# Part of wq in whole runs, eight partitions to a transfer, and the last piece of wo in two transfers

## Chip, cores, metric

The kernel runs on one core of a Trainium2 chip. The metric is the device time of one execution in microseconds, the median of several runs.

## The reference, cut to what matters

One decode step for a batch of 8: attention over the last 1,024 positions of a cache (16 query heads, 8 key/value heads, 256 wide), an MLP, and a gate that mixes the two.

```python
W = min(4096, max(256, Sk // 4))                 # 1024 of 4096 positions
q = (x @ wq) -> (B, Hq, 1, Dh)                   # x: 8 x 448, wq: 448 x 4096
k, v = last W positions, repeated for 2 query heads per kv head
o = softmax(q k^T * Dh**-0.5) v                  # per batch and head
a = o.reshape(B, Sq, Hq*Dh) @ wo                 # wo: 4096 x 448
b = gelu(layernorm(x) @ w1 + b1) @ w2 + b2
out = g * a + (1 - g) * b                        # g = sigmoid(sum(x * gate_w))
```

Everything is bf16. Keys and values alone are 64 transfers' worth of 1 MB; all weights together are some 10 MB.

## The kernel before

The order of work is written out by hand. Nearly all loads are issued by the sync engine (SP), in this order: w1 (L159, L162), w2 (L164), wq in three pieces (L167), the rest of wq (L168), and then the units of the list built at L170 to L179: a transfer of K or V for two batches of one kv head (1 MB, `load`, L148), and after each head's four K transfers the piece of wo that belongs to the head (448 KB, L187). Keys run ahead of values. The list ends with the last values and, as its last transfer, the piece of wo for the last head. The very last V transfer goes in two halves (L145). x, two biases and the gate's vector are issued by the scalar engine (L156 to L158, L288).

wq is 448 rows of 4,096 numbers. Its first 384 rows lie in `wq_sb` as 128 partitions of three rows: partition p holds rows 3p, 3p+1 and 3p+2, which are one run of 24,576 B in memory. Before, one transfer carries row c of every partition: 128 runs of 8,192 B, three transfers.

TensorE first makes the MLP's two products, then q (L377): for c = 0, 1, 2 and the rest, 32 small matmuls each, over all 128 partitions of `wq_sb[:, c]`. Then follows a software pipeline over 64 steps of half a K transfer each: transpose the keys (L407, copied out of PSUM by VectorE at L412), scores (L433), softmax once per head (L446 to L496), the values' product (L508), and per head the output product with wo (L533), which adds into one PSUM bank. For each head the output product takes the first query head's two blocks of wo, then the second's. At the end the last output product, one VectorE instruction (L577) and two stores (L581).

A pool of 12 buffers holds keys and values. The trace shows eight semaphore numbers on the loads, used in turn.

Of the kernel before, what the change touches and what calls it, by code (L numbers as in the profile page):

```python
# [16 lines left out]
def kernel(  # L17
# [15 lines left out]
    nc = tc.nc  # L33
    P = nc.NUM_PARTITIONS

    B, Sq, D = A_x.shape
    _, Hkv, Sk, Dh = A_k_cache.shape
    HD = A_wq.shape[1]
    Hq = HD // Dh
    rep = Hq // Hkv  # L40
# [4 lines left out]
    NJ = Dh // P  # L45
# [61 lines left out]
    NKH = rep * NJ  # L107
    wq_sb = big.tile([P, DC, HD], BF16, name="wq_sb")
    wq_t = big.tile([P, HH], BF16, name="wq_t")
    w1_sb = big.tile([P, DC, F], BF16, name="w1_sb")  # L110
    wo_sb = [big.tile([P, NKH, D], BF16, name=f"wo_sb{g}") for g in range(Hkv)]
# [29 lines left out]
    def load(kind, n):  # L141
        t = kvpool.tile([P, NC, Dh], BF16, tag="kv", name="kv")
        src = A_k_cache if kind == "K" else A_v_cache
        g, u = divmod(n, NBU)
        parts = TB if (kind, n) == ("V", NU - 1) else 1  # L145
        w = NC // parts
        for q in range(parts):
            nc.sync.dma_start(  # L148
                t[:, q * w : (q + 1) * w, :].rearrange("p c d -> p (c d)"),
                src[u * TB : (u + 1) * TB, g, kv0:Sk, :].rearrange(  # L150
                    "t (r c) d -> r t c d", c=NC
                )[:, :, q * w : (q + 1) * w, :].rearrange("r t c d -> r t (c d)"),
            )
        KV[kind, n] = t
# [8 lines left out]
    w2_v = w2_sb[:].rearrange("p (h k) n -> p h k n", h=2)  # L163
    nc.sync.dma_start(w2_v, B_w2.rearrange("(h p k) n -> p h k n", h=2, k=NH))  # L164
    wq_v = A_wq[0:DM, :].rearrange("(p c) n -> p c n", c=DC)
    for c in range(DC):
        nc.sync.dma_start(wq_sb[:, c, :], wq_v[:, c, :])  # L167
    nc.sync.dma_start(wq_t[:], A_wq[DM:D, :].rearrange("r (h n) -> (r h) n", h=2))  # L168

    VU = (SPG + LAG) // TB  # L170
# [11 lines left out]
    def issue_to(k):  # L182
        while pos[0] < len(units):
            kind, n = units[pos[0]]
            if kind == "W":
                r0 = n * NKH * P
                nc.sync.dma_start(  # L187
                    wo_sb[n][:].rearrange("p (i j) n -> p i (j n)", i=rep),
                    A_wo[r0 : r0 + NKH * P, :].rearrange(
                        "(i p j) n -> p i (j n)", i=rep, j=NJ  # L190
                    ),
                )
            else:
                if pos[1] == k:
                    return
                load(kind, n)
                pos[1] += 1
            pos[0] += 1

    issue_to(NKV)  # L200


# [343 lines left out]
    for n in range(LAST):  # L546
        if n < NSTEP:
            transposes(n)
            done += n % TB == TB - 1
        if 0 <= n - 1 < NSTEP:  # L550
            scores(n - 1)
        g, r = divmod(n, SPG)
        if g >= 1 and g - 1 < Hkv:
            if r == 0:
                soft_max1(g - 1)
            if r == 1:
                soft_max2(g - 1)
            if r == 2:
                soft_exp(g - 1)
        m = n - SPG - LAG  # L560
        if m >= 0:
            pv(m)
            if m % SPG == 1:
                soft_sum(m // SPG)
            if m == SPG:
                gate_load()
            if m == 2 * SPG:
                gate()
            done += m % TB == TB - 1
            if m % SPG == SPG - 1:  # L570
                o_scale(m // SPG)
            if m % SPG == 0 and m > 0:
                o_proj(m // SPG - 1)
        issue_to(NKV + done)
# [37 lines left out]
```

## Time and profile before

| what | value |
|---|---|
| median of 3 runs | 196.78 us (196.78 to 196.85) |
| the profiled execution: its time | 196.92 us |
| its span, first to last instruction | 195.2 us |
| moved by the DMA engines | 78.14 MB, 400 GB/s over the span |
| TensorE (PE) matmul busy | 164.2 us (84%) |
| VectorE (DVE) busy | 113.1 us (58%) |
| ScalarE (ACT) busy | 6.4 us (3%) |
| mean granted TensorE clock | 0.768 |

The profile gives, for each line of the kernel, the busy time and what an engine waited for; the span in 40 slices of 4.88 us with the share of the 16 DMA engines that were busy; the chain of waits that ended last; and for each window asked for, the busy time of each engine and the DMA share. Behind these views lie records of each DMA packet (start, length, bytes, queue) and of each landing: a transfer posts one landing on its semaphore for each DMA engine that carried a share of it.

### The profile page before, as it was taken

To read this page: it belongs to the slowest core of one execution; us is meant where nothing else is said; L and a number is where in the kernel's file an instruction comes from. 1 tells how busy PE (TensorE), PEld (TensorE's weight loads), DVE (VectorE), ACT (ScalarE), POOL (GpSimd) and SP (SyncE) were. 2 spreads that over 40 slices of the span, in tenths; PEclk is the share of its full clock that TensorE was granted. 3 is DMA by queue.
4 is the path that set the end of the run, shared out by engine and by line. 5 is a ranking of instruction groups with operands and counts; after the bars stand their busy time and mean duration, and the time that the engine had idled before them with its cause. 6 is when DMAs were issued, how large, how long until landed. Compare 5 with 4: busy or idle time off the path is not lost.

```text
span 195.2 us, 7355 instructions
## 1 busy us (share of the span) xinstructions
PE 164.2 (84%) x3417; PEld 153.6 (79%) x3417; DVE 113.1 (58%) x255; ACT 6.4 (3%) x13; POOL 2.8 (1%) x16
## 2 busy tenths in 40 slices
PE   2677799988899796958999898988898989989752
PEld 1565799988899796957999797978897989989541
DVE  3122189996477653764559674964586646766401
ACT  5000000000000000010000000000000000000000
POOL 5000000000000000000000000000000000000000
PEclk9999889997569855585569996995599655699555
DMA  6999999999999999999999999999999999999940
GB/s 215 412 426 425 425 413 426 426 423 420 421 426 422 417 425 426 425 417 431 423 423 419 422 425 428 418 421 418 425 430 417 421 425 430 426 420 425 394 176 5
DMA packets 12769, 78.14 MB, mean 400 GB/s; under 512 B 1330, under 2 KB 3523, under 8 KB 4164
## 3 DMA queue, kind: packets, MB, share of 16 engines
q1 hardware_dynamic: 12688, 77.67, 95.4%
q8 instruction: 26, 0.43, 0.8%
q10 hardware_dynamic: 52, 0.02, 0.0%
q14 instruction: 3, 0.02, 0.0%
HBM read 77.68 MB, written 0.01 MB: 398 GB/s over the span
## 4 chain that ended last, share of the span: by engine, by line
DMA 91%; PE 6%; SPq 1%; issue 0%; DVE 0%
DMA kv<-in_A_k_cache_dram 47%; DMA kv<-in_A_v_cache_dram 19%; DMA wo_sb<-in_A_wo_dram 18%; DMA wq_sb<-in_A_wq_dram 7%; PE ktp L407 4%; PE grp L433 1%; PE A_bank L533 0%; PE grp L508 0%; SPq L167 0%; PE grp L422 0%; SPq L164 0%; DVE res L577 0%; SPq L159 0%; SPq L162 0%; SPq L148 0%
## 5 line engine op out<-in xcount | busy, mean ns | idle before, releaser
L412 DVE COPY kt<-ktp 128x1024 bf16<-128x1024 bf16 x128 | 84.4, 687 | 44.4 <-PE ktp L407 43.9
L407 PE MATMUL ktp<-ident,kv 128*128 128x128 bf16 x1024 | 89.0, 257 | 7.9 <-DMA kv<-in_A_k_cache_dram 6.7
L407 PEld LDWEIGHTS <-kv 128*128 128x128 bf16 x1024 | 78.0, 118 | 10.9 <-DMA kv<-in_A_k_cache_dram 7.9
L508 PE MATMUL grp<-e,kv 128*128 128x4 bf16 x1024 | 35.6, 166 | 2.6 <-DMA kv<-in_A_v_cache_dram 2.5
L508 PEld LDWEIGHTS <-kv 128*128 128x128 bf16 x1024 | 32.6, 101 | 5.6 <-DMA kv<-in_A_v_cache_dram 2.8
L433 PE MATMUL grp<-qT,kt 128*128 128x4 bf16 x1024 | 36.6, 166 | 0.3 <-DVE kt L412 0.2
L433 PEld LDWEIGHTS <-kt 128*128 128x128 bf16 x1024 | 34.6, 100 | 1.8 <-issue 0.6
L482 ACT ACTIVATE e<-grp 128x256 bf16<-128x256 f32 x8 | 3.1, 383 | 161.8 <-PE grp L475 161.8
L491 PE MATMUL A_bank<-zs,onesf 128*128 128x16 f32 x16 | 3.6, 299 | 4.5 <-DVE zs L487 4.5
L491 PEld LDWEIGHTS A_bank<-zs,onesf 128*128 128x128 f32 x16 | 2.8, 218 | 5.1 <-DVE zs L487 5.1
L533 PE MATMUL A_bank<-wo_sb,ot 128*8 128x224 bf16 x64 | 5.5, 305 | 0.8 <-DMA wo_sb<-in_A_wo_dram 0.5
L321 PE MATMUL h_ps<-yT,w_sb 128*128 128x8 bf16 x42 | 4.2, 195 | 1.2 <-DMA w_sb<-in_B_w_dram 1.2
L495 DVE RECIPROCAL rz<-A_bank 128x16 f32<-128x16 f32 x8 | 2.1, 258 | 5.4 <-PE A_bank L491 5.4
L519 DVE TENSOR_TENSOR ot<-grp,rz 128x32 bf16<-128x32 f32 x8 | 1.5, 186 | 6.4 <-PE grp L508 6.4
L487 DVE TENSOR_REDUCE zs<-e 128x16 f32<-128x256 bf16 x8 | 4.8, 602 | 0.0
L353 PE MATMUL b_ps<-w_sb,hT 128*8 128x224 bf16 x28 | 2.8, 388 | 2.4 <-DVE b_ps L349 2.4
L338 DVE COPY z<-h_ps 128x112 f32<-128x112 f32 x1 | 0.3, 275 | 7.7 <-PE h_ps L329 7.7
L321 PEld LDWEIGHTS <-w_sb 128*128 128x128 bf16 x42 | 3.6, 152 | 1.3 <-DMA w_sb<-in_B_w_dram 1.3
L475 PE MATMUL grp<-diag,onesb 128*128 128x256 bf16 x8 | 2.5, 308 | 2.2 <-DVE diag L469 1.9
L353 PEld LDWEIGHTS <-hT 128*8 128x8 bf16 x28 | 1.8, 121 | 3.0 <-DVE hT L344 2.2
L446 DVE TENSOR_REDUCE pm<-grp 128x16 f32<-128x256 f32 x8 | 3.3, 415 | 0.6 <-PE grp L433 0.6
L533 PEld LDWEIGHTS <-ot 128*8 128x8 bf16 x64 | 2.6, 93 | 1.3 <-issue 0.4
(82 smaller groups left out, 53.6 us busy)
## 6 DMA issues: line engine op xcount, KB each, us to landing
kv<-in_A_k_cache_dram SPq DMA_DIRECT2D x32, 1024.0 KB, 18.3
kv<-in_A_v_cache_dram SPq DMA_DIRECT2D x31, 1024.0 KB, 18.3
wo_sb<-in_A_wo_dram SPq DMA_DIRECT2D x8, 448.0 KB, 18.3
wq_sb<-in_A_wq_dram SPq DMA_DIRECT2D x3, 1024.0 KB, 12.1
w_sb<-in_B_w_dram SPq DMA_DIRECT2D x1, 1568.0 KB
w_sb<-in_B_w_dram SPq DMA_DIRECT2D x1, 1344.0 KB, 5.9
kv<-in_A_v_cache_dram SPq DMA_DIRECT2D x2, 512.0 KB, 19.8
wq_t<-in_A_wq_dram SPq DMA_DIRECT2D x1, 512.0 KB, 14.5
```

What stands on the lines that cost most here:

```text
L321: nc.tensor.matmul(o, lhsT=cols(w1_sb[:, c, h * FH : (h + 1) * FH]), rhs=yT[:, c, :], start=(c == 0), stop=False,)
L353: nc.tensor.matmul(b_ps[CP * j : CP * j + NB, 0:DN], lhsT=M["hT"][:, k * NB : (k + 1) * NB] if k < NF else onesb[0:1, 0:NB], rhs=w2_sb[:, ...
L407: nc.tensor.transpose(ktp[:, c * P : (c + 1) * P], K[:, h * HC + c, j * P : (j + 1) * P], ident[:],)
L412: nc.vector.tensor_copy(kt[:, j, :], ktp[:])
L433: nc.tensor.matmul(G[g][:, s : s + RU], lhsT=kt[:, j, c * P : (c + 1) * P], rhs=qT[:, j, g, bu * TB : (bu + 1) * TB, :].rearrange("p t i - ...
L446: nc.vector.reduce_max(pm[:], G[g][:, S0 : S0 + NC * R].rearrange("p (c r) -> p r c", r=R), axis=AXIS.X,)
L475: nc.tensor.matmul(G[g][:, S0 : S0 + NC * R].rearrange("p (c r) -> p c r", c=NC), lhsT=onesb[:], rhs=diag[g % 2][:].unsqueeze(1).to_broadc ...
L482: nc.scalar.activation(e[:], G[g][:, S0 : S0 + NC * R], ACT.Exp)
L487: nc.vector.reduce_sum(zs[:], E[g][:].rearrange("p (c r) -> p r c", r=R), axis=AXIS.X)
L491: nc.tensor.matmul(zc, lhsT=onesf[:], rhs=zs[:], start=False, stop=True, skip_group_check=True)
L508: nc.tensor.matmul(G[g][:, o : o + RU], lhsT=V[:, cc, :].rearrange("p (q j) -> p j q", j=NJ)[:, j, :], rhs=E[g][:, cc * R + bu * RU : cc * ...
L533: nc.tensor.matmul(A_bank[CP * j : CP * j + NB, 0:DN], lhsT=ot[:].rearrange("p j (b i) -> p j i b", i=rep)[:, h, i, :], rhs=wo_sb[g][:, k, ...
```

## The change

Of the 128 partitions of `wq_sb`, the last 48 (80 to 127) are loaded in six transfers of eight partitions, each partition as its whole run of 24,576 B (196,608 B to a transfer). Two of these go ahead of each of the three transfers that carry row c, which now carry it for partitions 0 to 79 only. The piece of wo for the last head is issued as two transfers, one per query head, where it was one. The bytes that are loaded and where they lie in SBUF stay the same.

```diff
     wq_v = A_wq[0:DM, :].rearrange("(p c) n -> p c n", c=DC)
+    SH = 48
+    PM = P - SH
+    small = [(p, p + 8) for p in range(PM, P, 8)]
     for c in range(DC):
-        nc.sync.dma_start(wq_sb[:, c, :], wq_v[:, c, :])
+        for lo, hi in small[2 * c : 2 * c + 2]:
+            nc.sync.dma_start(
+                wq_sb[lo:hi].rearrange("p c n -> p (c n)"),
+                wq_v[lo:hi].rearrange("p c n -> p (c n)"),
+            )
+        nc.sync.dma_start(wq_sb[0:PM, c, :], wq_v[0:PM, c, :])
     nc.sync.dma_start(wq_t[:], A_wq[DM:D, :].rearrange("r (h n) -> (r h) n", h=2))
...
             if kind == "W":
                 r0 = n * NKH * P
-                nc.sync.dma_start(
-                    wo_sb[n][:].rearrange("p (i j) n -> p i (j n)", i=rep),
-                    A_wo[r0 : r0 + NKH * P, :].rearrange(
-                        "(i p j) n -> p i (j n)", i=rep, j=NJ
-                    ),
+                dst = wo_sb[n][:].rearrange("p (i j) n -> p i (j n)", i=rep)
+                src = A_wo[r0 : r0 + NKH * P, :].rearrange(
+                    "(i p j) n -> p i (j n)", i=rep, j=NJ
                 )
+                if n < Hkv - 1:
+                    nc.sync.dma_start(dst, src)
+                else:
+                    for i in range(rep):
+                        nc.sync.dma_start(dst[:, i, :], src[:, i, :])
```

## The prediction

> **What bounds the kernel now.** I read the page's slices and queue table first:
>
> ```profile
> DMA  6999999999999999999999999999999999999940
> GB/s 215 412 426 425 425 413 426 426 423 420 421 426 422 417 425 426 425 417 431 423 423 419 422 425 428 418 421 418 425 430 417 421 425 430 426 420 425 394 176 5
> ...
> q1 hardware_dynamic: 12688, 77.67, 95.4%
> q8 instruction: 26, 0.43, 0.8%
> ```
>
> The 16 DMA engines are busy from the second slice to the 38th at some 424 GB/s; PE is busy for 84%. Then the rate drops to 394 and 176 with work still to do. Besides the loads, queue q8 fetches instructions: 26 packets of 16 KB. The chain of waits, its end:
>
> ```profile
> 136.11 18.32 DMA wo_sb<-in_A_wo_dram
> 154.44 0.02 issue
> 154.45 0.02 SPq L148
> 154.47 0.03 issue
> 154.50 19.52 DMA kv<-in_A_k_cache_dram
> 174.01 0.02 issue
> 174.03 17.30 DMA wo_sb<-in_A_wo_dram
> 191.33 0.04 issue
> 191.37 0.93 PE A_bank L533 x8
> 192.30 0.02 issue
> 192.32 0.44 DVE res L577
> ```
>
> Loads are 91% of the chain. Each is issued as an earlier one lands (eight semaphores in turn: SP waits until the transfer eight before has landed on every engine). The last link is the last piece of wo, landing at 191.33; behind it lie 0.93 us of L533 and the end. So the time is that of the DMA engine that finishes last. The windows of the tail show how uneven they are (after PE to POOL come the clock, the DMA share and GB/s):
>
> ```profile
> 184.00:185.00 1.00, 1.00 (x23) 0.62 (x19) 0.00 (x0) 0.00 (x0) 0.00 (x0) 0.50 0.92 374
> 185.00:186.00 1.00, 1.00 (x28) 1.00 (x26) 0.26 (x1) 0.00 (x0) 0.00 (x0) 0.50 0.60 245
> ...
> 188.00:189.00 1.00, 0.81 (x31) 0.72 (x27) 0.00 (x0) 0.00 (x0) 0.00 (x0) 0.50 0.47 187
> 189.00:190.00 1.00, 0.59 (x16) 0.51 (x16) 0.00 (x0) 0.00 (x0) 0.00 (x0) 0.50 0.29 112
> 190.00:191.00 1.00, 0.58 (x16) 0.50 (x16) 0.14 (x1) 0.00 (x0) 0.00 (x0) 0.50 0.08 29
> ```
>
> From 185 on half of the engines are done (share 0.60 to 0.47). The 16 landings of the last wo piece say it exactly: seven engines at 184.98 to 185.71, one at 186.86, six at 189.63 to 189.89, one at 190.66, one at 191.33. I followed each engine through the packet records (on a busy engine a packet starts within a few ns of where the one before ended: a K row of 8,192 B every 306 ns, 26.8 B/ns). The eight late engines are those that took the 26 fetches, in turn, three or four each; a fetch puts an engine back by some 1.5 us. An even split would be worth at most some 3.6 us (mean of the 16 landings 187.8).
>
> **Which engines the new transfers use.** The trace has transfers to eight partitions:
>
> ```profile
> x_sb<-in_A_x_dram ACTq DMA_DIRECT2D x1, 7.0 KB
> ...
> gw_sb<-in_gate_w_dram ACTq DMA_DIRECT2D x1, 7.0 KB
> ```
>
> Each has eight data packets of 896 B on eight engines, one partition each. Following gw_sb's packets at 63.27 to 63.53, six sit on early engines and two on late ones: one that ends near 189.8, and the one with four fetches that ends at 190.66. So the new transfers shift load from one set of eight engines to another, but that set is not the idle one. (The Trainium skill, "DMA: Bandwidth & Descriptors", section on the semaphore's 16, says that such a transfer runs on the eight lowest-numbered engines; the eight landings of gw_sb agree with the eight, their numbers no row shows.)
>
> **Part by part.**
>
> *Bytes per engine.* Before, each engine carries 24 rows of wq: 24 x 306 ns = 7.3 us. After, every engine carries 3 x 5 rows (80 partitions over 16): 15 x 306 = 4.6 us, and the set of eight also six pieces of 24,576 B.
>
> *One piece.* Lower bound: the engine's own speed in a K load, 24,576 / 26.8 = 0.92 us. But eight engines now write into eight neighbouring partitions at once, which no long transfer of the trace does. In K loads eight partitions take 8 x 8,192 B in 8 x 306 ns, 26.8 B/ns in all, one engine's worth; if neighbours take no more than that, a piece lasts 7.34 us. x_sb speaks against so much: 7,168 B into eight partitions, first packet at 1.77, last landing 2.24; at 26.8 B/ns the data alone would need 0.27 us, and with the 0.31 to 0.34 us that a landing follows its semaphore packet in K loads the last would be at 2.35 or later. At twice that rate (0.13 us) it fits, and with no limit at all it also fits (its last packet ends at 1.89). So a piece costs between 0.92 and 3.67 us. I take 3.67: 896 B are little enough to be absorbed on the way, whereas the K rows, a third of a piece in size and sustained, never put more than one engine's worth into eight partitions. The Trainium skill, "SBUF — State Buffer", section Door 1, speaks against the change: eight neighbouring partitions from a multiple of eight reach two of 16 ports, each about 27 GB/s; 196,608 B through two would by estimate take 3.6 us, and the sum would be the one below within half a microsecond.
>
> *The eight engines:* 6 x 3.67 + 4.6 = 26.6 us where there were 7.3: +19.3 us. The latest of the set ended at 190.66, so 209.9; the last landing moves from 191.33 by +18.6 us. If 80 partitions also crowd the write side (eight rows of 306 ns where there are five, three times), 2.7 us more; if a fetch falls into a stalled stretch and costs nothing, 1.5 us less.
>
> *Who waits.* q (L377) needs all rows of `wq_sb[:, c]`, so all six new transfers; it starts at some 36 us instead of 18.73, takes 3.6 us and is over before the first K, which moves from 23.50 to some 42. PE then runs at the DMA's pace as before; early slack doesn't matter.
>
> *SP.* Seven more issues of 0.3 to 0.5 us, at the head beside w1 and w2, which keep the engines busy until 10.4 us. The third row transfer now waits for the first new one to land, and wq_t, K and the rest queue behind it on SP. With fast pieces that landing is near 11.6, the first packet some 1.0 us after (w1: issued 0.80, first packet 1.84), and the engines outside the set have rows until some 13.4: covered, with about 0.8 us to spare, and only what goes beyond that would cost. With slow pieces they run dry, but they are not the ones that end last.
>
> *wo in two.* The second piece lands when the one transfer did. The first four matmuls need only the first, half of 16 x 71 ns earlier, so they start when ot is ready (191.05 to 191.11) and not at 191.37: -0.26 us, between 0 (if all eight wait for both) and that.
>
> **Sum.** 196.92 (span 195.2 and 1.7 around it) + 18.6 - 0.3 = 215.2; the median of the runs is 0.14 below the profiled time: 215.1. Own range with the two corrections, 213 to 219.
>
> **Rivals.**
>
> *Pieces at full speed, the same eight engines.* The piece costs 0.92 us, the set carries 6 x 0.92 - 2.75 = +2.76 us. The late engine at 190.66 goes to 193.4, +2.1 us; less 0.26: 198.6. For it: the 896 B packets were as long (39 to 69 ns) as a lone one (41). It ends slower because the set holds two fetching engines.
>
> *Pieces at full speed, on the eight engines without fetches (faster).* The set is read from the scalar engine's queue; SP could use another. Then the early ones go to at most 186.86 + 2.76 = 189.6, the others to 191.33 - 2.76 = 188.6: -1.7, less 0.26, 194.8. PE would allow it: from 183.0 on it has some 6 us of work. It is faster only while 186.86 + 6 pieces - 2.75 stays under 191.33, a piece below 1.2 us. Against it: two of eight in gw_sb.
>
> *The change doesn't do what it says:* each run of 196,608 B is cut over all 16 engines and nothing is moved between them: 196.5.
>
> **How the numbers follow.** Slow pieces 0.50; full speed on the mixed set 0.24; something between or beyond, mostly slower, 0.04; full speed on the free set 0.18; nothing moved 0.04. So slower 0.78, faster 0.18, within 0.2% (about what a measurement of this kernel can tell) 0.04. The value is that of the first case. The range goes from the case with nothing moved, 196.5, to 219 and leaves out the faster case.
>
> **What would show it.** Right: the DMA share falls to about 0.6 or less for many microseconds between 14 and 37, q's matmuls start near 36, the first K lands near 42, and the tail's uneven end is as long or longer. Packets of 24,576 B would last 3 to 4 us; 0.92 us would prove the main step wrong. If they last 0.92, the tail decides: a share near 0.06 to 0.12 until 193 is the mixed set, all engines done by 190 the free one. In both, the last L533 should show no wait of 0.5 us for wo_sb.

## The result and the profile after

The change makes the kernel slower: 217.43 us (median, 216.62 to 219.61) against 196.81 us, ratio 1.1064 (95% interval 1.0983 to 1.1145). The forecast was 215.1 us, range 196.5 to 219. The profiled execution after took 217.19 us, its span is 215.3 us.

The page's DMA slices of the changed kernel (slices of 5.4 us here) show where the time went: six slices, from the third to the eighth, move 93 to 365 GB/s. From the ninth on the rate is again that of before.

```profile
DMA  6999898999999999999999999999999999999940
GB/s 231 422 117 183 93 184 105 365 419 426 420 419 425 422 426 421 420 425 424 420 423 425 419 427 422 425 422 418 424 422 429 418 423 428 423 423 422 383 164 11
...
q1 hardware_dynamic: 12656, 77.67, 95.5%
q8 instruction: 26, 0.43, 0.7%
```

Bytes and fetches are the same. In windows of 5 us (after POOL: clock, DMA share, GB/s):

```profile
10.00:15.00 5.00, 3.13 (x35) 2.81 (x33) 1.33 (x6) 0.30 (x1) 0.00 (x0) 1.00 1.09 163
15.00:20.00 5.00, 3.05 (x30) 1.87 (x30) 0.83 (x3) 0.00 (x0) 0.00 (x0) 1.00 1.17 198
20.00:25.00 5.00, 0.00 (x0) 0.00 (x0) 0.00 (x0) 0.00 (x0) 0.00 (x0) 1.00 0.86 88
25.00:30.00 5.00, 0.00 (x0) 0.00 (x0) 0.00 (x0) 0.00 (x0) 0.00 (x0) 1.00 1.15 195
30.00:35.00 5.00, 0.00 (x0) 0.00 (x0) 0.00 (x0) 0.00 (x0) 0.00 (x0) 1.00 0.96 98
```

The share stays near 1 while the bytes fall to between a fifth and a half of the 424 GB/s before: the engines are "busy" with packets that don't get through. PE idles for 20.7 us on wq. q starts at 39.3 us where it started at 18.7 (the second line is from the list of what its engine sat idle for):

```profile
L391 PE MATMUL q_ps<-xT,wq_sb x96: 166/168/189, 39.3 to 41.9; 128*128 128x8 bf16 x96
...
  DMA wq_sb<-in_A_wq_dram: 20.7, 1
```

The first K lands on its last engine at 44.42 (before: 23.50). The end of the chain of waits, and the tail's windows:

```profile
208.60 2.55 PE grp L522 x96
211.16 0.02 issue
211.18 0.20 DVE ot L533
211.38 0.04 issue
211.43 0.93 PE A_bank L547 x8
212.36 0.02 issue
212.38 0.44 DVE res L591
```

```profile
208.00:209.00 1.00, 1.00 (x29) 1.00 (x27) 0.26 (x1) 0.00 (x0) 0.00 (x0) 0.50 0.15 62
209.00:210.00 1.00, 1.00 (x44) 1.00 (x42) 0.00 (x0) 0.00 (x0) 0.00 (x0) 0.50 0.13 54
210.00:211.00 1.00, 1.00 (x43) 1.00 (x40) 0.00 (x0) 0.00 (x0) 0.00 (x0) 0.50 0.12 47
```

From 208 on some two engines of 16 still work (share 0.12 to 0.15), until the last wo piece lands at 211.45. TensorE, at half clock (0.50 in these windows), is by then as late as they are: its last output product (L547) starts at 211.43. So the chain names TensorE and not the DMA.

The packet records give the new packets' own time. The 48 pieces (a piece is one partition's run of 24,576 B) took 1.57 to 3.83 us; in pairs of transfers (mean over the eight engines) 2.35 and 2.93, then 2.99 and 3.70, then 2.97 and 3.65 us.

### The profile page after: what moved, and what is told of

Same layout as the page of the kernel before. It is cut to its first block, busy times and chain, and to the rows that moved or that the text cites. A ratio compares the mean times of both kernels' runs of the same rounds, so it can differ in the third digit from the quotient of the medians.

```text
span 215.3 us, 7365 instructions
## 1 busy us (share of the span) xinstructions
PE 164.6 (76%) x3417; PEld 153.6 (71%) x3417; DVE 113.2 (53%) x255; ACT 6.4 (3%) x13; POOL 2.8 (1%) x16
## 4 chain that ended last, share of the span: by engine, by line
DMA 51%; PE 37%; DVE 8%; issue 2%; SPq 0%; ACT 0%; ACTq 0%
DMA kv<-in_A_k_cache_dram 33%; PE ktp L421 21%; DMA wq_sb<-in_A_wq_dram 13%; PE grp L447 6%; PE grp L522 5%; DMA w_sb<-in_B_w_dram 5%; DVE kt L426 4%; PE q_ps L391 2%; PE A_bank L547 2%; PE A_bank L505 1%; DVE zs L501 1%; DVE diag L483 1%; PE grp L436 0%; PE grp L489 0%; DVE pm L460 0%
## 5 line engine op out<-in xcount | busy, mean ns | idle before, releaser
L391 PE MATMUL q_ps<-xT,wq_sb 128*128 128x8 bf16 x96 | 2.8, 168 | 20.7 <-DMA wq_sb<-in_A_wq_dram 20.7
L391 PEld LDWEIGHTS <-wq_sb 128*128 128x128 bf16 x96 | 2.7, 104 | 21.0 <-issue 20.9
L403 DVE TENSOR_SCALAR qT<-q_ps 128x128 bf16<-128x128 f32 x2 | 0.5, 298 | 27.0 <-PE q_ps L391 27.0
L547 PE MATMUL A_bank<-wo_sb,ot 128*8 128x224 bf16 x64 | 6.2, 335 | 0.5 <-DVE ot L533 0.3
```

Source lines behind the costliest of these rows:

```text
L391: nc.tensor.matmul(q_ps[:, k * NB : (k + 1) * NB], lhsT=w, rhs=xs, start=(c == 0 and k == 0), stop=(c == DC), skip_group_check=True,)
L547: nc.tensor.matmul(A_bank[CP * j : CP * j + NB, 0:DN], lhsT=ot[:].rearrange("p j (b i) -> p j i b", i=rep)[:, h, i, :], rhs=wo_sb[g][:, k, ...
```

## The experiments

There were three theories beforehand. (1) The write side: neighbours among the partitions share a way in. (2) The read side: eight engines get in each other's way on one run of memory. (3) Long packets on eight engines are slow as such.

**Target and source apart.** Three kernels, run on the same chip. The first spreads both:

```diff
-        for lo, hi in small[2 * c : 2 * c + 2]:
+        for i in range(2 * c, 2 * c + 2):
+            lo, hi = small[i]
...
-                wq_sb[lo:hi].rearrange("p c n -> p (c n)"),
-                wq_v[lo:hi].rearrange("p c n -> p (c n)"),
+                wq_sb[PM + i : P : 6].rearrange("p c n -> p (c n)"),
+                wq_v[PM + i : P : 6].rearrange("p c n -> p (c n)"),
```

> The changed kernel, but each of the six transfers takes every sixth partition of 80 to 127 instead of eight neighbours (the same rows in the same partitions, the same 24,576 B runs, eight partitions to a transfer). Theory 1, the write side: eight neighbouring partitions take only about two engines' worth of data, so spread pieces run at 0.92 us each, at most 1.84 where two of the eight share a path; the first K lands by some 25 us and the time is that of the rival with the mixed set, 198.6 us (197.5 to 201). Theory 2, the read side: eight engines that read one run of 196,608 B get in each other's way; here the runs are apart in memory too, so also about 198.6. Theory 3: pieces of 24,576 B on eight engines are slow wherever they lie: 217 us as the changed kernel.

The second has only the `wq_v` line spread, the third only the `wq_sb` line.

> The changed kernel with only the source spread: the eight neighbouring partitions of a transfer get the rows of every sixth partition of 80 to 127 (so the rows of wq in these partitions are permuted against x: this kernel computes another q, and its time alone is of use). Theory 1 (write side): pieces of 2.9 to 3.8 us, 217 us. Theory 2 (read side): pieces near 0.92 us, some 198.6 us. Theory 3 (length): 217 us.

> The changed kernel with only the destination spread: one run of 196,608 B of memory goes to every sixth partition of 80 to 127 (rows permuted against x as in the run before). Theory 1 (write side): pieces of 0.92 to 1.84 us, some 198.6 us. Theory 2 (read side): 217 us. Theory 3 (length): 217 us.

| the six transfers | time, us | piece, us (mean of each transfer) |
|---|---|---|
| changed kernel: neighbours from neighbours | 217.43 | 2.35 to 3.70 |
| source apart, target neighbours | 218.21 (one run) | 2.67 to 4.00 |
| target apart, source neighbours | 207.82 (one run) | 1.23 to 2.11 |
| both apart | 209.82, ratio 1.0678 (1.0656 to 1.0700) | 1.46 to 2.15 |

It is the target that decides, not the source, and not the packets' length: theories 2 and 3 fall. That the kernel with only the target apart is 2 us faster than the one with both apart rests on one run and isn't explained. But the full speed of 0.92 us isn't reached, and the forecast of 198.6 for spread targets missed by 11 us. With both apart the first windows read:

```profile
10.00:15.00 5.00, 3.11 (x35) 2.79 (x33) 1.35 (x6) 0.30 (x1) 0.00 (x0) 1.00 1.03 242
15.00:20.00 5.00, 3.06 (x30) 1.90 (x30) 0.82 (x3) 0.00 (x0) 0.00 (x0) 1.00 0.97 211
20.00:25.00 5.00, 0.00 (x0) 0.00 (x0) 0.00 (x0) 0.00 (x0) 0.00 (x0) 1.00 1.12 259
```

about half of the rate of before, over the same stretch. Something besides the pieces is slow, and the packet records show the 8,192 B rows of the 80-partition transfers at some 0.56 us where they took 0.31. By estimate the six pieces account for 5.2 us of the miss (10.7 us in all in place of 5.5) and the 15 rows of an engine for 3.8.

**The row half by itself.** Theory 1 now has three forms: (1a) only partitions that share a way in slow each other; (1b) an engine is slow outside the partitions that it serves in a transfer of 128; (1c) any transfer that isn't 128 partitions wide is slow. The first kernel has no long runs and no transfer on eight engines; each row transfer goes in two:

```diff
-        nc.sync.dma_start(wq_sb[:, c, :], wq_v[:, c, :])
+        for lo, hi in ((0, 80), (80, P)):
+            nc.sync.dma_start(wq_sb[lo:hi, c, :], wq_v[lo:hi, c, :])
```

> The kernel before with each of wq's three row transfers cut in two, partitions 0 to 79 and 80 to 127 (8,192 B rows, no whole runs, all 16 engines on each). It prices the row half of the change by itself. Theory 1a (shared destinations): eight of the 80 partitions share one, so 2.45 us for five rows to an engine where 1.53 would do, and eight of the 48 too, 2.45 us for three: 14.7 us for wq instead of 7.3, at most +7.4 us on all engines alike, 204.2 us; less if the two transfers overlap on different destinations. A theory without a limit on the write side: 196.8 us.

And the same cut by parity:

```diff
-        nc.sync.dma_start(wq_sb[:, c, :], wq_v[:, c, :])
+        for h in range(2):
+            nc.sync.dma_start(wq_sb[h:P:2, c, :], wq_v[h:P:2, c, :])
```

> The kernel before with each of wq's three row transfers cut in two by parity: the even partitions and the odd ones (64 partitions each, spread over the whole height; all 16 engines, four rows each). Theory 1a: as many rows per shared destination as in one transfer of 128, so no or little loss: 196.8 to 199 us. Theory 1b and 1c (engines away from home, or any transfer that isn't 128 wide, at half speed): 24 rows at 0.55 instead of 0.31 us, +5.9 us, 202.7 us.

Windows of the first (80 and 48), then of the second (even and odd):

```profile
10.00:15.00 5.00, 3.17 (x36) 2.86 (x34) 1.29 (x6) 0.30 (x1) 0.00 (x0) 1.00 1.06 247
15.00:20.00 5.00, 3.97 (x62) 2.77 (x62) 0.88 (x3) 0.00 (x0) 0.00 (x0) 1.00 1.02 213
20.00:25.00 5.00, 0.94 (x32) 0.88 (x32) 0.00 (x0) 0.00 (x0) 0.00 (x0) 0.74 0.99 212
```

```profile
10.00:15.00 5.00, 3.20 (x36) 2.89 (x35) 1.26 (x5) 0.30 (x1) 0.00 (x0) 1.00 1.01 426
15.00:20.00 5.00, 4.38 (x82) 3.30 (x83) 0.90 (x3) 0.00 (x0) 0.00 (x0) 1.00 1.03 431
20.00:25.00 5.00, 3.98 (x98) 3.83 (x96) 1.09 (x3) 0.00 (x0) 0.00 (x0) 1.00 1.01 421
```

204.32 and 196.75 us (one run each). Both have six transfers where there were three, on all 16 engines. The first fits a cost by the count of rows that fall to one group of eight partitions (204.2 was the estimate, its upper bound); in the second, 64 partitions spread over the whole height cost nothing, and wq's rows took 0.309 us (the longest 0.324). So neither the number of transfers nor a width other than 128 is the cause: theories 1b and 1c fall. By the Trainium skill, "SBUF — State Buffer", section Door 1, partitions share 16 ports in groups that repeat every 32 partitions within each half of 64. Both times agree with this rule. Of the pieces in the changed kernel only the longer transfers do, at 3.65 and 3.70 us against an estimate of 3.6 for two ports; the other four transfers took 2.35 to 2.99 us.

**Sixteen to a transfer.**

```diff
-    small = [(p, p + 8) for p in range(PM, P, 8)]
+    small = [(p, p + 16) for p in range(PM, P, 16)]
...
-        for lo, hi in small[2 * c : 2 * c + 2]:
+        for lo, hi in small[c : c + 1]:
```

> The changed kernel with sixteen neighbouring partitions to a transfer, three transfers of whole runs instead of six, so that all 16 engines carry one piece each of every transfer. Theory 1a (shared destinations): sixteen neighbours are four engines' worth, 3.67 us a piece as in the changed kernel; per engine 3 x 3.67 for the pieces and 15 rows at the measured 0.56 to 0.58 us, 19.6 us instead of 7.3: +12.3 us, 208.8 us, and the tail as uneven as before (no engine carries more than another). A theory by which eight engines are the cause (half of the engines idle, the other half overloaded): pieces near 0.92, some 199 us.

207.21 us (one run), near the 208.8 of theory 1a and far from 199. The pieces took 1.84 to 3.06 us, shorter than the 3.67 expected and two to three times 0.92: they are slow though all 16 engines carry the same, so idle engines are not what makes them slow. From landing to landing (medians of the 16 engines) a transfer of sixteen takes 3.1 to 3.3 us. The eight-engine transfers are thus dearer by 10 us than the same bytes in transfers of sixteen neighbours.

**The pieces at the other end.** Partitions 0 to 47 instead of 80 to 127:

```diff
-    small = [(p, p + 8) for p in range(PM, P, 8)]
+    small = [slice(j, 32, 4) for j in range(4)] + [slice(32 + j, SH, 2) for j in range(2)]
...
-        nc.sync.dma_start(wq_sb[0:PM, c, :], wq_v[0:PM, c, :])
+        nc.sync.dma_start(wq_sb[SH:P, c, :], wq_v[SH:P, c, :])
```

> The changed kernel with the other end of the partitions: the six transfers of whole runs take partitions 0 to 47, the first four of them every fourth of 0 to 31 (one partition out of each group of four), the last two every second of 32 to 47; the row transfers take 48 to 127. Spread over 80 to 127 a piece took 1.7 us, not 0.92, and the rows of the 80 partitions 0.56 us, not 0.31. Theory 1a, only shared destinations slow anything, and groups of four that lie 32 apart share one: here the first four pieces and the other engines' rows don't meet, so 0.92 us a piece and 0.31 to 0.49 a row, some 199 to 203 us. Theory 1b, an engine outside the partitions that it serves in a 128-partition transfer runs at half speed: the first four pieces, each at home on its engine, take 0.92, the rows 0.55, some 203 to 206 us. Theory 1c, any transfer that isn't 128 partitions wide runs at half speed: pieces 1.7, rows 0.55, as spread over 80 to 127: 208 to 210 us.

206.03 us (one run), outside the 199 to 203 us of theory 1a. All eight pieces of the first transfer took 0.912 us: the lower bound of the prediction is real, an engine does pass a run of 24,576 B at 26.9 B/ns. It also says that pieces four partitions apart share no way in that limits them. Only that transfer was so fast; the following ones took 1.22, 1.41, 1.39, 1.67 and 1.88 us. In the last two, two pieces fall to each group, for which theory 1a gives up to 1.84. The 1.2 to 1.4 us of the others it doesn't explain.

The row transfer isn't as separate from the pieces as the expectation says: partitions 48 to 63 lie 32 above 16 to 31 and would share their groups. But all eight pieces of the second transfer took 1.16 to 1.31 us, those to partitions below 16 too. Nor is a row transfer beside them enough: between 10.26 and 10.54 us eight other engines began its rows, while the pieces of the fast first transfer ran until 11.29, and up to 10.87 these rows took 0.309 us as well. From about then on, rows and newly started pieces slow down together. What slows pieces on eight different groups stays open, here and in the spread kernels; pieces without any row transfer beside them weren't tried.

**The wo half alone.** The kernel before with only the second half of the change's diff.

> The kernel before with only the last piece of wo in two transfers. By the prediction the first four of the last output product's matmuls start at 191.1 and not at 191.37: -0.26 us, 196.5 us. A rival: the matmuls wait for both pieces all the same, 196.8 us, or the extra transfer delays the landing by its own issue, up to +0.4 us.

196.46 us, ratio 0.9988 (0.9980 to 0.9997). The chain's end:

```profile
171.46 18.70 DMA kv<-in_A_v_cache_dram
...
190.21 0.60 PE grp L514 x16
...
191.08 0.93 PE A_bank L539 x8
...
192.03 0.44 DVE res L583
```

The wait for wo_sb ahead of the last output product is gone; V is the last load on the chain. This is the best version of the study, by 0.3 us.

**The wq half alone.** The change's first half, wo in one transfer.

> Only the wq half of the change, the last piece of wo in one transfer as before. The wo half alone gave -0.3 us at the end of the chain, where the last landing sets the end: 217.7 us if the tail is the same here. A rival: in the changed kernel TensorE is late at the end (it ends 212.4, the last wo landed at 211.45), so that the split is worth nothing there: 217.4 us. One run can't tell 0.3 us apart; it tells whether the wq half is the whole of the loss, within 1 us.

219.03 us in the one run, above both expected times; the changed kernel's own runs span 216.62 to 219.61. The wq half is the whole of the loss, as far as one run tells. What the split of wo is worth in the changed kernel this run can't tell.

**An attempt to level the engines otherwise.** To the kernel with wo's last piece in two, half of the first wo piece goes over partition counts that put it on six engines:

```diff
-                if n < Hkv - 1:
-                    nc.sync.dma_start(dst, src)
-                else:
+                if n in (0, Hkv - 1):
                     for i in range(rep):
-                        nc.sync.dma_start(dst[:, i, :], src[:, i, :])
+                        cuts = (0, 114, 120, P) if (n, i) == (0, 0) else (0, P)
+                        for lo, hi in zip(cuts, cuts[1:]):
+                            nc.sync.dma_start(dst[lo:hi, i, :], src[lo:hi, i, :])
+                else:
+                    nc.sync.dma_start(dst, src)
```

> An attempt at a version that beats both. The kernel before with the last wo piece in two (which gave 196.46), and half of the first wo piece (partitions of the first query head, 1,792 B each) moved to fewer engines by its partition count: 114 partitions, whose largest divisor up to 16 is 6, then 6, then 8. If these six are among the early engines, they carry some 21 packets of 1,792 B more in place of 8 (+1.0 us at full speed, +2.2 at half), and the late ones 8 less (-0.57): 195.9 us. If a fetching engine is among the six: 196.5 to 198. The packets also show whether six engines in neighbouring blocks of 19 partitions run at full speed (74 ns) or at half.

198.17 us (196.84 to 199.30), ratio 1.0065 (1.0039 to 1.0090): slower by 0.65%. The transfer did run on six engines (six landings). From 29.4 to 31.4 us nearly all 1,792 B packets took 81 to 140 ns in place of 74, and the rate dipped (the same two windows before read 419 and 423 GB/s):

```profile
25.00:30.00 5.00, 5.00 (x100) 4.78 (x99) 4.18 (x8) 0.00 (x0) 0.00 (x0) 1.00 1.02 396
30.00:35.00 5.00, 5.00 (x127) 5.00 (x125) 4.98 (x9) 0.00 (x0) 0.00 (x0) 1.00 1.02 381
```

The execution that this trace shows took 196.97 us, though, no longer than the kernel before: the dip is shown, the cause of the slower executions isn't. One reading of the dip, which no run here tests, is that every group of partitions is already being filled at its full rate, so that an engine that writes elsewhere takes from another.

## Why the prediction was right, step by step

- *What bounds it, and which engines.* Right. The 16 landings of the last wo piece after are two at 201.25 and 201.72, six at 205.56 to 206.97, six at 207.09 to 208.84, two at 211.26 and 211.45. These are the numbers of the mixed set read from gw_sb: two early engines outside the set, six fetching ones outside it, six early ones in it (before: 184.98 to 186.86, so +22), and the two fetching ones in it, which end the kernel as forecast.
- *One piece.* The step that carried the forecast, that eight neighbours take in less than eight engines send, was right: with the target apart the pieces fall to 1.23 to 2.11 us. Its size, 3.67 us, was the upper bound of what the prediction's rows allowed. It held for the second transfer of the later pairs (3.70, 3.65) and was too large for the others; the six came to 18.6 us on an engine, not 22.0.
- *The rows* were mis-sized the other way: five rows took 3.4 to 3.6 us (means, from the end of a pair of pieces to the start of the next), not 1.53; the correction named for it gave 2.45. Three times that is some 10.4 us in place of 4.6. The set's wq thus took some 29 us, not 26.6. That the forecast came within 2.3 us is in part luck: 3.4 us too much for the pieces, 5.8 too little for the rows.
- *The sum.* The last landing moved by 20.1 us (211.45 against 191.33), +18.6 were forecast. 196.92 + 20.1 is 217.0, without any gain from the split of wo; the profiled run took 217.19. One correction, a fetch that falls into a stalled stretch, fits: the set's engines are 21.8 us late with wq_t (41.15 against 19.31, medians) and the last of them 20.8 at the end.
- *Who waits.* q from 39.3, not 36; first K at 44.4, not 42. "Early slack doesn't matter" was nearly too simple: TensorE starts 21 us later, and at the end it is as late as the DMA.
- *wo in two.* -0.32 us by itself, -0.26 forecast. In the changed kernel the term was worth next to nothing: the last output product started at 211.43, only 0.02 us ahead of wo's last landing at 211.45.
- *What would show it.* One sign was read wrongly beforehand: the DMA share did not fall to 0.6, it stayed at 0.86 to 1.17 in the windows of 5 us above, since packets that wait count as busy. GB/s showed it. The pieces lasted 1.57 to 3.83 us, not 3 to 4.
- *The rivals.* A gain needed pieces below 1.2 us on the set without fetches; the landings show the mixed set, and even spread over 48 partitions the transfers' means were 1.23 to 2.15. The packets of 24,576 B on eight engines rule out that nothing was moved.

## What to carry to other kernels

In these runs a transfer's speed depended on how its partitions lie over the whole height, more than on its length or its count of engines. So cut a load by parity (here free) or by columns (the wo half), not into blocks of neighbouring partitions. Read GB/s beside the DMA share: a share of 1 with a quarter of the rate means packets that are stuck. Uneven engines (here 3.6 us at the end) weren't levelled by transfers on fewer engines: the one attempt, on six, lost 0.65%.

## What the runs showed that was not expected

- Rows of 80 neighbouring partitions take some 0.56 us instead of 0.31, and cutting wq's rows at partition 80 costs 7.5 us by itself (204.32 against 196.82). Rows of 64 partitions two apart take 0.309 us and cost nothing.
- Spread pieces took 1.2 to 2.1 us (means of a transfer); only the first transfer of the kernel with pieces four partitions apart ran at 0.912 us. Why stays open.
